# Attention and a feed-forward block on one core: the first stage keeps the feed-forward of one chunk only, and all other chunks run by seven products

## The chip, the cores and the metric

The kernel runs on one core of a Trainium2 chip. The metric is the device time of one launch in microseconds; the median of three runs before the change is 1090.41 us (1090.18 to 1091.8).

## The reference, cut to what matters

```python
# 8 batches x 8 heads x 576 tokens, head_dim 64, 128 features; all fp32
def phi(x):
    proj = np.einsum('bhsd,df->bhsf', x, w_phi)
    proj = proj - np.max(np.abs(proj), axis=-1, keepdims=True)
    return np.concatenate([np.exp(proj), np.exp(-proj)], axis=-1)
q_p, k_p = phi(q), phi(k)
kv  = np.einsum('bhsf,bhsd->bhfd', k_p, v)
z   = np.sum(k_p, axis=2)
num = np.einsum('bhsf,bhfd->bhsd', q_p, kv)
den = np.einsum('bhsf,bhf->bhs', q_p, z)[..., None] + 1e-06
x   = (num / den) as 4608 tokens x 512          # heads side by side
h   = x @ w_in                                  # 512 x 2048
g   = np.maximum(h, 0.0) + alpha * np.minimum(h, 0.0)
out = g @ w_out                                 # 2048 x 512
```

## The kernel before, in words

**Attention.** Work goes by head pairs, 32 of them (`attention_units`, i = 0 to 31): 576 tokens of two heads, keys and queries side by side as nine blocks of 128 tokens. Per pair TensorE projects to 128 features (`project`, L357, tiles `pj` and `pl`: 18 matmuls, each run as two instructions, as all fp32 matmuls here but the transposes), VectorE finds the largest magnitude of each token and subtracts it (L361, L362, result `t`), ScalarE takes both exponentials (L375, L370 for keys). TensorE then sums the key features with a matrix of ones (`k_z`, L415) and multiplies them with v (`k_acc`, L398), both into one PSUM tile `kv`; ScalarE copies it out (`ks`), TensorE transposes it (`kt`, L430), ScalarE copies it (`sf`). Query features are transposed (`q_turn`, L444 and L441, tiles `qt`), and ScalarE takes their exponentials on the way out of PSUM (`qf`, L454, L452). Numerator and denominator are matmuls of `sf` with `qf` (`num`, L463; `den`, L481). The denominator goes through DRAM: row `d9`, reciprocal on VectorE (L500), `rec_d`, a broadcast load `rr`; GpSimd multiplies (L513), and the result is stored to `x_d`.

For the first nine pairs (`ZP`) the sum over tokens takes 20 matmuls with ones. From pair 9 on VectorE first adds the features of the token blocks (`k_sum`, L384, L388, L391, tiles `y` and `z`), and four matmuls are left.

**Precision.** Feed-forward operands are split into a high part and a rest (`rnd`, L154; `low`, L158), so each product is three matmuls (high x high, rest x high, high x rest) of 128 x 128 weights and 512 tokens. The weights arrive as 64-bit words: 32 blocks (16 tiles of d_ff, in and out), each taken apart by ScalarE (scale), four VectorE operations (L206, L207, L213, L214), a GpSimd addition (L218), a ScalarE cast and a GpSimd subtraction.

**Feed-forward.** 4608 tokens are nine chunks of 512. A chunk and one d_ff tile of 128 cost 4 x 3 matmuls up and 4 x 3 down when done plainly. Stage 1 does four of the 16 tiles (`NF1`) plainly for every chunk; chunks 0 to 6 are spread between the attention of later pairs (`ffn1_units`), and the partial outputs go to `part_d` in DRAM. After the last pair comes a stretch of plain work: chunk 0's other twelve tiles (`up2`, `down2`, weights loaded back from DRAM, tile `wd`) and the four tiles of chunks 7 and 8. The last stage takes chunks 1 to 8 in four pairs of chunks and the remaining twelve tiles in pairs (`unit`, `down_pair`): a 2 x 2 block product by seven products and not eight, 42 matmuls up and 42 down for two tiles and two chunks. Its operands are sums and differences of activation blocks (`prepare`, `piece`, tiles `xo`; `operand`, tiles `hv`) and of weight blocks (`sums`: stored to `us_d`, `vs_d`). `sums` reads the decoded weights back from `a_d` and runs on VectorE, after attention.

**What sets the order.** TensorE, SyncE's DMA queue, VectorE and ScalarE follow a list `todo` of (time, function), sorted by hand-tuned times (`places`, `F0` to `U10`, one unit is one pair); after attention the list binds TensorE and SyncE, and in the last stage TensorE, SyncE and GpSimd.

Of the kernel before, what the change touches and what calls it, by code (L numbers as in the profile page):

```python
# [61 lines left out]
ZP = 9


def places(i):
    early = i < ZP
    end = i >= NPAIR - 2
    first = {}
    if i == 0:
        first = dict(  # L70
            kz=0.6087, ka=0.708, ko=0.7486, kr=0.9934, kc=1.4482,
            n=1.9214, q=(0.8813, 0.8308, 0.8837), qe=(0.9994, 1.6727, 0.9984),
        )
    if i == 1:
        first = dict(kz=0.0042, ka=0.0046, ko=0.005)
    return dict(
        ld=-2.0487,
        lv=-0.6714,
        p=(-0.9958 if early else -0.997, -0.2212),
        pl=-0.2217,  # L80
        ke=(-0.1643, -0.0046),
        ks=(-0.1042, 0.1628, 0.3174),
        kz=0.9909,
        ka=1.0012,
        ko=1.0069,
        kr=1.0717,
        kc=1.1318,
        q=(1.4145, 1.4146, 1.3876),
        qe=(1.416, 1.4689, 1.4006),
        d=1.9929,  # L90
        ds=2.0026,
        n=2.0048,
        s=2.0313,
        d9=2.3018,
        dv=2.7654 if early else 2.9056 if end else 2.6473,
        rd=2.9221 if early else 3.2095 if end else 2.7929,
        rr=3.2932 if early else 3.4567 if end else 2.924,
        x=3.3204 if early else 3.4698 if end else 3.4373,
        xs=3.799 if early else 3.7869 if end else 3.541,
    ) | first  # L100


F0 = 9.2903
FR = 3.3778
FB = 8.0905
FL = 1.3973
FX = (1.1204, 0.6722, 0.1849, 0.3895)
FX0 = (1.6389, 1.8451, 1.1996, 0.5009)
FX1 = (0.7187, 0.4692, 0.2819, 0.3079)
FL0 = 2.0983  # L110
FG = (0.1212, 0.3467, 0.482)
GL = (0.3336, 0.4933, 0.5782)
GT = (0.1537, 0.1934, 0.4757)
GE = (0.2092, 0.3109, 0.5393)
# [1066 lines left out]
```

## Time and profile before

| | |
|---|---|
| median of three runs | 1090.41 us |
| the profiled execution, first to last instruction | 1086.2 us |
| TensorE busy | 1060.3 us (98%) |
| VectorE busy | 814.3 us (75%) |
| ScalarE busy | 622.8 us (57%) |
| GpSimd busy | 248.2 us (23%) |
| moved by DMA | 252.18 MB |

The page states no time of the profiled execution besides its span; the median of the runs stands 4.2 us above it. Busy times are unions of an engine's records, so matmuls that overlap count once, and the mean of one matmul is longer than the step from one start to the next. The attention stage with its interleaved feed-forward ends near 477 us, the last seven-product stage begins at 614 us.

### The profile page before, as it was taken

What the parts mean: (1) busy time and instruction counts of PE and PEld (TensorE: products, weight loads), DVE (VectorE), ACT (ScalarE), POOL (GpSimd) and SP (SyncE); (2) the same over time, 40 slices, a digit from 0 to 9 for tenths busy, and PEclk for the clock granted to TensorE, in tenths of its full rate; (3) what the DMA queues carried; (4) which work ended last, traced back from release to release, by engine and by line L of the source; (5) the groups of instructions that cost most, each with busy time, mean ns of one, the idle gap of its engine ahead of it and who ended that gap; (6) DMA issues with size and microseconds to landing.
All of it is one profiled execution on the core that took longest, in us unless ns stands there. A gap on an engine that the chain in (4) does not pass through costs nothing. (4 is left out here: it accounts for less than half of the span.)

```text
span 1086.2 us, 18393 instructions
## 1 busy us (share of the span) xinstructions
PE 1060.3 (98%) x6958; PEld 815.2 (75%) x6958; DVE 814.3 (75%) x1204; ACT 622.8 (57%) x1177; POOL 248.2 (23%) x251
## 2 busy tenths in 40 slices
PE   8999999999999999989897999999999999999998
PEld 6767677677667766767676877888888888888886
DVE  7877889798898988563655578975697669766784
ACT  5777676686667767654544446553565346444542
POOL 1334152424334352442411001012001200020001
PEclk9999999999999999989998999999999999999999
DMA  5576556657666675679579689487657756675555
GB/s 187 184 225 174 152 193 206 228 189 255 192 213 231 219 239 177 199 265 376 185 251 361 249 300 403 161 307 262 225 216 264 276 211 248 223 279 209 193 179 179
DMA packets 97703, 252.18 MB, mean 232 GB/s; under 512 B 17616, under 2 KB 18000, under 8 KB 92240
## 3 DMA queue, kind: packets, MB, share of 16 engines
q1 hardware_dynamic: 84400, 197.46, 53.4%
q0 software_dynamic: 12928, 53.48, 13.6%
q8 instruction: 55, 0.90, 0.3%
q14 instruction: 32, 0.26, 0.1%
q10 hardware_dynamic: 288, 0.07, 0.0%
HBM read 190.91 MB, written 59.92 MB: 231 GB/s over the span
## 5 line engine op out<-in xcount | busy, mean ns | idle before, releaser
L154 ACT CAST hv<-g 128x512 fp32r<-128x512 f32 x168 | 103.8, 622 | 88.6 <-DVE hv L158 29.8
L158 DVE TENSOR_TENSOR hv<-g,hv 128x512 fp32r<-128x512 f32 x168 | 114.4, 688 | 38.5 <-ACT hv L154 38.1
L361 DVE TENSOR_REDUCE m<-pj 128x8 f32<-128x1024 f32 (+1 forms) x66 | 78.3, 1187 | 32.6 <-PE pj L357 32.4
L806 POOL DMA_DIRECT2D out_dram<-pt x33 | 18.0, 547 | 356.7 <-DVE pt L935 355.0
L513 POOL TENSOR_TENSOR s<-s,rr 128x576 f32<-128x576 f32 x32 | 46.7, 1461 | 159.7 <-DMA rr<-rec_d 113.7
L362 DVE TENSOR_TENSOR t<-pj,m 128x1024 f32<-128x1024 f32 (+1 forms) x66 | 78.7, 1192 | 3.3 <-ACT s L474 0.5
L281 DVE SCALAR_TENSOR_TENSOR g<-r,aln,g 128x512 f32<-128x512 f32 x48 | 43.3, 902 | 44.4 <-ACT g L277 44.2
L921 PE MATMUL qa<-hv,wv 128*128 128x512 f32 x192 | 74.8, 390 | 0.0
L919 PE MATMUL qa<-hv,wv 128*128 128x512 f32 x192 | 74.7, 389 | 0.0
L920 PE MATMUL qa<-hv,wv 128*128 128x512 f32 x192 | 74.7, 389 | 0.0
L357 PE MATMUL pj<-w_sb,raw 64*128 64x128 f32 x1024 | 71.7, 279 | 2.1 <-DVE t L362 1.2
L357 PEld LDWEIGHTS pj<-w_sb,raw 64*128 64x128 f32 x1024 | 62.6, 188 | 14.3 <-issue 11.8
L454 ACT ACTIVATE qf<-qt 128x512 f32<-128x512 f32 x128 | 68.7, 618 | 1.4 <-PE qt L444 1.4
L463 PE MATMUL n<-qf,sf 128*64 128x288 f32 x512 | 69.0, 412 | 0.0
L375 ACT ACTIVATE xk<-t 128x1024 f32<-128x1024 f32 x64 | 64.9, 1077 | 5.2 <-DVE t L362 5.2
L218 POOL TENSOR_TENSOR aw<-ew,aw 128x512 f32<-128x512 f32 x32 | 44.6, 1394 | 89.4 <-DVE ew L214 89.4
L563 PE MATMUL o<-gh,w 128*128 128x512 f32 x144 | 62.0, 430 | 2.7 <-ACT gh L154 2.5
L565 PE MATMUL o<-gl,w 128*128 128x512 f32 x144 | 58.6, 407 | 4.4 <-DVE gl L158 4.2
L398 PE MATMUL kv<-xk,v 128*64 128x256 f32 x512 | 62.3, 385 | 0.0
L554 PE MATMUL h<-xh,w 128*128 128x512 f32 x144 | 60.4, 419 | 0.0
L564 PE MATMUL o<-gh,w 128*128 128x512 f32 x144 | 58.1, 404 | 0.0
L474 ACT COPY s<-n 128x288 f32<-128x288 f32 x64 | 25.1, 400 | 56.1 <-PE n L463 42.4
(193 smaller groups left out, 2816.7 us busy)
## 6 DMA issues: line engine op xcount, KB each, us to landing
ws<-us_d SPq DMA_DIRECT2D x24, 1024.0 KB
wv<-vs_d SPq DMA_DIRECT2D x32, 768.0 KB
wv<-v_d SPq DMA_DIRECT2D x24, 768.0 KB
raw<-kq_dram SPq DMA_DIRECT2D x31, 576.0 KB
wa<-u_d SPq DMA_DIRECT2D x24, 512.0 KB
v<-v_dram SPq DMA_DIRECT2D x32, 320.0 KB
xr<-x_d SPq DMA_DIRECT2D x10, 1024.0 KB
rr<-rec_d SPq DMA_DIRECT2D x64, 144.0 KB
```

What stands on the lines that cost most here:

```text
L154: return act.copy(dst, src)
L158: return eng.tensor_tensor(dst, src, f(hi), op=ALU.subtract)
L357: pe.matmul(dst[h, j], lhsT=c["raw"][hs, ts], rhs=w_sb[hs], start=True, stop=True)
L361: dve.tensor_reduce(m, src, axis=AX.X, op=ALU.max, apply_absolute_value=True)
L362: dve.tensor_tensor(t[:, hs, js], src, m.unsqueeze(3).broadcast_to([P, nh, nj, FD]), op=ALU.subtract)
L375: act.activation(x[:, a], c["t", 0], AF.Exp, scale=sg)
L398: pe.matmul(c["kv"][h * D : (h + 1) * D, 0:2], lhsT=c["v"][:, tp, h, :], rhs=c["x", ch][:, :, h, j, :], start=tp == 0, stop=tp == NV - 1,)
L454: act.activation(c["qf"][:, h, a, : 4 * P], ps.rearrange("p j f -> p (j f)"), AF.Exp, scale=sg)
L463: pe.matmul(ps[h * D : (h + 1) * D, :], lhsT=c["st"][:, a, h * D : (h + 1) * D], rhs=c["qf"][:, h, a, u * HS : (u + 1) * HS], start=a == 0 ...
L919: pe.matmul(ps, lhsT=wh, rhs=xh, start=first, stop=False, skip_group_check=True)
L920: pe.matmul(ps, lhsT=wl, rhs=xh, start=False, stop=False, skip_group_check=True)
L921: pe.matmul(ps, lhsT=wh, rhs=xl, start=False, stop=end, skip_group_check=True)
```

## The change

- Stage 1 keeps the feed-forward of chunk 0 alone, with all 16 tiles (`first_chunk`): 32 visits of twelve matmuls (one tile up, or two output blocks of a tile pair down), in slots 8 to 28; even slots have two visits, odd ones one (`SL`). A slot is the work between two projections. Outputs are added up in SBUF by VectorE (`down0_out`). The stretch between attention and the last stage, `part_d`, `a_d` and the plain weights read back are gone.
- Chunks 1 to 8 run all 16 tiles, eight units for a chunk pair and not six, by seven products. Weight sums for all eight are made on GpSimd during attention, as soon as a block pair is decoded (`sum_two` to `sum_rest`), and stored by SyncE.
- In a slot TensorE does one burst of 36 projection instructions of the next pair, one visit of 128x32 matmuls (ones, v, numerator of the pair before, denominator: `k_acc` and `num` now write 32 rows at a time), and one run of transposes. The projected queries are centred and transposed in the slot of their projection. `k_sum` is gone.
- The projection's `pl_0`, the last query transposes `q2` and the denominator share one PSUM bank (tag `a`); `kv` and `kt` share one; `num` uses the bank pair of the keys' projection.
- GpSimd now follows the list too; `places` is replaced by one table of offsets (`OFF`, in fourteenths of a slot, for slots with no, one and two visits) and `PE_AT` for TensorE. In the last stage there are five `hv` tiles (`NH`), and weights arrive for two units at a time in five buffers.

```diff
-NF1 = 4
-NF2 = NF - NF1
-NU = NF2 // 2
+NU = NF // 2
...
-NH = 6
+NH = 5
...
+SL = [sl for sl in range(8, 29) for _ in range(2 - sl % 2)]
+DS = [sl for sl in range(26) for _ in range(2 if sl in (8, 10, 12, 14, 16, 18) else 1)]
...
+PE_AT = dict(pk=0.0, kz=2.0, ka=3.0, n=5.2, d=7.15, kr=8.1, q=8.4, f0=9.95, f1=12.7)
...
+    def sum_two(u, z):
...
+        pool.tensor_tensor(a22, a21, a22, op=ALU.add)
+        pool.tensor_tensor(a21, a11, a21, op=ALU.subtract)
+
+    def sum_four(u, z):
+        _, a11, a12, a21, a22 = wst["s", u, z]
+        pool.tensor_tensor(a11, a22, a11, op=ALU.subtract)
+        pool.tensor_tensor(a12, a12, a11, op=ALU.subtract)
...
+    def sum_rest(u, z):
...
+        low(pool, dst[:, :, 1], st[0], dst[:, :, 0])
...
+        def project():
+            for ch in range(2):
+                p2 = c["pj", ch] = ps_pj.tile([P, 2, 4, FD], F32, tag=f"p{ch}", name=f"pj{i}_{ch}")
+                for j in range(4):
+                    for h in range(2):
+                        project_one(p2[:, h, j], h, 5 * ch + j)
+            c["pl"] = [
+                ps_m.tile([P, 1, 1, FD], F32, tag="a", name=f"pl{i}_0"),
+                psf.tile([P, 1, 1, FD], F32, tag=ftag(1), name=f"pl{i}_1"),
+            ]
+            for h in range(2):
+                project_one(c["pl"][h][:, 0, 0], h, 4)
...
         def k_acc():
             for tp in range(NV):
                 ch, j = divmod(tp, 4)
-                for h in range(2):
+                for g in range(4):
+                    h, e = divmod(g, 2)
                     pe.matmul(
-                        c["kv"][h * D : (h + 1) * D, 0:2],
-                        lhsT=c["v"][:, tp, h, :],
+                        c["kv"][32 * g : 32 * g + 32, 0:2],
+                        lhsT=c["v"][:, tp, h, 32 * e : 32 * e + 32],
                         rhs=c["x", ch][:, :, h, j, :],
...
-            if i < ZP:
-                zs = [c["x", 0][:, :, :, j, :] for j in range(4)] + [c["x", 1][:, :, :, 0, :]]
-            else:
-                zs = [c["z"]]
+            zs = [c["x", 0][:, :, :, j, :] for j in range(4)] + [c["x", 1][:, :, :, 0, :]]
...
+        put(i - 1, "pk", project)
+        put(i - 1, "mk", lambda: centre_four(0))
+        put(i - 1, "mq", lambda: centre_four(1))
+        put(i - 1, "mt", centre_tails)
...
+        put(i - 1, "q", q_turn)
+        put(i - 1, "qe", q_exp)
+        put(i, "kz", k_z)
+        put(i, "ka", k_acc)
...
+        put(i + 1, "n", num)
+        put(i + 1, "d", den)
...
+    def down0_out(u, m):
+        if u == 0:
+            o0[m] = cat.tile([P, C2], F32, name=f"os0_{m}")
+            act.copy(o0[m], cur[m])
+            return
+        dve.tensor_tensor(o0[m], cur[m], o0[m], op=ALU.add)
...
+    def first_chunk():
+        order = [("u", 0), ("u", 1)]
+        for k in range(NU - 1):
+            order += [("u", 2 * k + 2), ("d", k, 0), ("u", 2 * k + 3), ("d", k, 2)]
+        order += [("d", NU - 1, 0), ("d", NU - 1, 2)]
...
+    pinned = {et.PE, et.SP, et.DVE, et.Activation, et.Pool}
```

**TensorE, one pair without feed-forward.** Before, from one sum with ones to the next (`xk` and `k` are key features, `raw` the loaded tokens):

```order
L415 MATMUL kv_964<-xk_805,ones 32x128 x16
L415 MATMUL kv_964<-k_1_138,ones 32x128 x4
L481 MATMUL d_985<-qf_908,sf_892 32x288 x8
L398 MATMUL kv_964<-xk_805,v_750 64x256 x8
L398 MATMUL kv_964<-k_1_138,v_750 64x256 x2
L357 MATMUL pj_0_1011<-w_sb,raw_812 128x128 x8
L463 MATMUL n_0_1023<-qf_908,sf_892 64x288 x4
L463 MATMUL n_1_1028<-qf_908,sf_892 64x288 x4
L430 MATMUL kt_1038<-ident,ks_1033 128x128 x3
L441 MATMUL qt_2_1054<-ident,t_1_780 128x128 x2
L444 MATMUL qt_0_1061<-ident,t_1_780 128x128 x4
L444 MATMUL qt_1_1066<-ident,t_1_780 128x128 x4
```

And now, from one projection to the next:

```order
L370 MATMUL pj_0_322<-w_sb,raw_184 128x128 x8
L370 MATMUL pj_1_331<-w_sb,raw_184 128x128 x8
L370 MATMUL pl_0_340<-w_sb,raw_184 128x128
L370 MATMUL pl_1_341<-w_sb,raw_184 128x128
L428 MATMUL kv_349<-xk_281,ones 32x128 x16
L428 MATMUL kv_349<-k_1_129,ones 32x128 x4
L414 MATMUL kv_349<-xk_281,v_163 32x256 x16
L414 MATMUL kv_349<-k_1_129,v_163 32x256 x4
L479 MATMUL n_404<-qf_246,sf_346 32x288 x16
L496 MATMUL d_437<-qf_246,sf_346 32x288 x8
L443 MATMUL kt_450<-ident,ks_448 128x128 x3
L458 MATMUL qt_1_455<-ident,t_1_425 128x128 x4
```

The projection, which stood in two places with 128x64 matmuls between, is one burst; all matmuls of 32 columns follow one another; the transposed queries (`t_1_425`) are those of the burst at the head of the same slot.

**VectorE, the beginning of a slot with two visits, now** (`g_6`, `gl_6` are chunk 0's activation and its rest, `os` its output, `m` the magnitudes, `a` a weight block):

```order
L308 SCALAR_TENSOR_TENSOR g_6_3099<-r_6_3098,aln,g_6_3099 128x512
L610 TENSOR_TENSOR os_0_2171<-o_2_0_3139,os_0_2171 128x512
L388 TENSOR_REDUCE m_0_3255<-pj_0_3174 128x8
L389 TENSOR_TENSOR t_0_3254<-pj_0_3174,m_0_3255 128x1024
L388 TENSOR_REDUCE m_1_3279<-pj_1_3183 128x8
L389 TENSOR_TENSOR t_1_3278<-pj_1_3183,m_1_3279 128x2x512
L388 TENSOR_REDUCE m_2_3289<-pl_0_3192 128x1
L389 TENSOR_TENSOR t_1_3278<-pl_0_3192,m_2_3289 128x128
L388 TENSOR_REDUCE m_3_3292<-pl_1_3193 128x1
L389 TENSOR_TENSOR t_1_3278<-pl_1_3193,m_3_3292 128x128
L161 TENSOR_TENSOR gl_6_3316<-g_6_3099,gh_6_3204 128x512
```

All centring of a pair stands in one piece behind the addition of the last output block and ahead of the remaining feed-forward and weight work of the slot.

**GpSimd, about one slot with two weight blocks, now** (`e` and `a` are the parts of a weight block, `wo` its split form, `sd` the split sums, `s` a pair's numerator):

```order
L161 TENSOR_TENSOR sd_1_2879<-a_1_2454,sd_1_2879 128x4x256
L228 TENSOR_TENSOR a_0_2629<-e_0_2921,a_0_2629 128x512
L228 TENSOR_TENSOR a_1_2871<-e_1_2924,a_1_2871 128x512
L161 TENSOR_TENSOR wo_0_3036<-a_0_2629,wo_0_3036 128x2x256
L161 TENSOR_TENSOR wo_1_3038<-a_1_2871,wo_1_3038 128x2x256
L528 TENSOR_TENSOR s_2478<-s_2478,rr_2977 128x576
L256 TENSOR_TENSOR a_0_2629<-a_0_2629 128x256
L257 TENSOR_TENSOR a_0_2629<-a_0_2629 128x256
```

Before, GpSimd had the additions, the split and the multiplication here; the sums (L256, L257 and `sd`) stood on VectorE after attention.

## Rows read from the trace of the kernel before

**Rows 1.** The page's first line and its line of busy time: busy us, share of the span, instructions of each engine.

```profile
span 1086.2 us, 18393 instructions
PE 1060.3 (98%) x6958; PEld 815.2 (75%) x6958; DVE 814.3 (75%) x1204; ACT 622.8 (57%) x1177; POOL 248.2 (23%) x251
```

**Rows 2.** Busy time of each engine by stretch: stretch in us from the span's start, its length, then busy us and instructions of TensorE, its weight loads, VectorE, ScalarE and GpSimd; the granted clock of TensorE as a share of full speed; the DMA engines' share; GB/s.

```profile
0.00:42.74 42.74, 38.55 (x477) 28.98 (x478) 33.83 (x58) 25.50 (x52) 9.49 (x15) 1.00 0.58 188
42.74:95.62 52.88, 52.88 (x708) 37.40 (x706) 41.77 (x66) 40.54 (x88) 23.11 (x18) 1.00 0.66 205
300.00:400.00 100.00, 100.00 (x878) 70.02 (x878) 90.40 (x120) 69.80 (x142) 39.32 (x27) 1.00 0.70 222
477.00:490.00 13.00, 8.96 (x25) 5.99 (x24) 8.20 (x11) 3.74 (x7) 6.51 (x6) 0.74 0.59 205
535.00:545.00 10.00, 7.14 (x23) 4.77 (x21) 6.72 (x8) 5.17 (x9) 6.53 (x6) 0.83 0.51 171
583.00:595.00 12.00, 5.57 (x17) 4.15 (x16) 7.22 (x12) 3.64 (x6) 1.24 (x2) 0.72 0.95 346
614.00:1081.20 467.20, 464.46 (x2042) 382.34 (x2040) 349.96 (x553) 232.17 (x395) 40.97 (x74) 1.00 0.68 244
```

**Rows 3.** TensorE's timeline over one pair without feed-forward: start in us, duration of the merged group, line, operation, tiles, shape, count.

```profile
42.74 1.08 PE L415 MATMUL kv<-xk,ones 128*32 128x128 f32 x32
...
43.86 1.15 PE L481 MATMUL d<-qf,sf 128*32 128x288 f32 x16
44.94 1.95 PE L398 MATMUL kv<-xk,v 128*64 128x256 f32 x16
...
47.25 1.16 PE L357 MATMUL pj<-w_sb,raw 64*128 64x128 f32 x16
48.34 2.16 PE L463 MATMUL n<-qf,sf 128*64 128x288 f32 x16
50.43 0.55 PE L430 MATMUL kt<-ident,ks 128*128 128x128 f32 x3
...
52.00 0.49 PE L357 MATMUL pl<-w_sb,raw 64*128 64x128 f32 x4
...
53.32 0.32 PE L415 MATMUL kv<-xk,ones 128*32 128x128 f32 x4
```

**Rows 4.** The same timeline over a later pair: from its numerator to the next one's, with the first and the last of the 24 feed-forward matmuls between, and the step with ones.

```profile
246.04 2.16 PE L463 MATMUL n<-qf,sf 128*64 128x288 f32 x16
...
248.43 0.48 PE L563 MATMUL o<-gh,w 128*128 128x512 f32 x1
...
256.45 0.39 PE L565 MATMUL o<-gl,w 128*128 128x512 f32 x1
256.77 0.43 PE L415 MATMUL kv<-z,ones 128*32 128x128 f32 x8
257.02 1.15 PE L481 MATMUL d<-qf,sf 128*32 128x288 f32 x16
...
261.50 0.71 PE L463 MATMUL n<-qf,sf 128*64 128x288 f32 x4
```

**Rows 5.** The same timeline in the seven-product stage: two matmuls ten starts apart.

```profile
700.28 0.39 PE L919 MATMUL qa<-hv,wv 128*128 128x512 f32 x1
...
702.55 0.39 PE L920 MATMUL qa<-hv,wv 128*128 128x512 f32 x1
```

**Rows 6.** The same timeline behind two of TensorE's waits (in brackets the idle time before the matmul and what ended it): the first and the last of thirteen matmuls behind one of them, and the first behind another.

```profile
482.95 0.80 PE L565 MATMUL o<-gl,w 128*128 128x512 f32 x1 [3.15 <-DVE gl L158]
...
488.23 0.56 PE L565 MATMUL o<-gl,w 128*128 128x512 f32 x1
...
590.53 0.77 PE L563 MATMUL po<-gh,wd 128*128 128x512 f32 x1 [6.43 <-DMA wd<-v_d]
```

**Rows 7.** Groups of VectorE and ScalarE instructions by line and shape: line, engine, operation, tiles, shape, count, busy us in total, mean ns of one, and the engine's idle time before them with what ended it.

```profile
L158 DVE TENSOR_TENSOR hv<-g,hv 128x512 fp32r<-128x512 f32 x168 | 114.4, 688 | 38.5 <-ACT hv L154 38.1
L281 DVE SCALAR_TENSOR_TENSOR g<-r,aln,g 128x512 f32<-128x512 f32 x48 | 43.3, 902 | 44.4 <-ACT g L277 44.2
L158 DVE TENSOR_TENSOR gl<-g,gh 128x512 fp32r<-128x512 f32 x48 | 36.7, 767 | 12.1 <-ACT gh L154 12.0
L207 DVE SCALAR_TENSOR_TENSOR aw<-raww,aw 128x512 uint32<-128x512 uint32 x32 | 26.3, 822 | 1.1
L388 DVE TENSOR_TENSOR z<-y 128x512 f32<-128x512 f32 x23 | 25.8, 1124 | 0.1
L214 DVE SCALAR_TENSOR_TENSOR ew<-raww,ew 128x512 f32<-128x512 uint32 x32 | 22.2, 692 | 1.1
L206 DVE TENSOR_SCALAR aw<-aw 128x512 uint32<-128x512 uint32 x32 | 21.5, 673 | 13.8 <-ACT aw L198 12.7 <-DMA part_d<-os 1.1
L213 DVE TENSOR_SCALAR ew<-aw 128x512 uint32<-128x512 uint32 x32 | 16.3, 511 | 3.0 <-DVE aw L207 0.5
L454 ACT ACTIVATE qf<-qt 128x512 f32<-128x512 f32 x128 | 68.7, 618 | 1.4 <-PE qt L444 1.4
```

**Rows 8.** The same for GpSimd's addition of weight parts.

```profile
L218 POOL TENSOR_TENSOR aw<-ew,aw 128x512 f32<-128x512 f32 x32 | 44.6, 1394 | 89.4 <-DVE ew L214 89.4
```

More of the change, by code (lines that the diff above doesn't have):

```diff
@@ L57 @@
 RAW_BUFS = 2
-S_BUFS = 2
-GB = 5
-XR_BUFS = 1
+S_BUFS = 4
 QH_BUFS = 2
[L62 to L100, printed above, removed]
@@ L103 @@
[L103 to L114, printed above, removed]
-TL = 31.4
-WL = dict(load=-1.1556, scale=-0.4743, split=-0.0175, rest=0.0884, add=0.3177, high=0.7022, low=0.9429, store=1.0847)
-FS = (0.0611, 0.2856)
-GV = 0.4491
-WT = dict(load=-0.63, scale=-0.2464, split=-0.0569, rest=0.0013, add=0.3952, high=0.6164, low=0.8038, store=1.0429)
@@ L256, in fused_kernel, with decode_at @@
     )
-    def decode_at(t, blk):
-        return [(t + (WT if t < TL else WL)[k], lambda u=u: u(*blk, WD)) for k, u in stages.items()]
-    inplace = {(ff, z) for ff in range(NF1) for z in range(2)}
-    W = {ff: weight_tile(w1p, f"w{ff}")[0] for ff in range(NF1)}
-    last = [None]
-    newest = {}
-    def behind(eng):
-        return tc.issue_after(newest[eng].ins)
+    def decode_at(sl, turn, ff, z):
+        for k, u in stages.items():
+            put(sl - (k == "load") + (k == "store"), k, lambda u=u: u(ff, z), turn)
+        if ff % 2:
+            for n, (u, ds) in enumerate(((sum_two, 1), (sum_four, 1), (sum_high, 1), (sum_rest, 1), (sum_store, 1))):
+                put(sl + ds, f"sum{n}", lambda u=u: u(ff // 2, z), turn)
     def act_g(ps, ff, n, gp, rg, bufs, tag, el, g_bufs=G_BUFS):
@@ new lines, in down0, with out0 @@
+    def down0(u, m, two):
+        cur[m] = ps = bank0(m + 1, two, f"o0_{u}_{m}")
+        for r in range(2):
+            gemm2(ps, weights_of(2 * u + r, 1), m, *gq[2 * u + r], r == 0, r == 1)
+    def down0_out(u, m):
[4 more added lines that the diff above has]
+        dve.tensor_tensor(o0[m], cur[m], o0[m], op=ALU.add)
+    def out0(m):
+        nc.sync.dma_start(out[m * P : (m + 1) * P, :C2], o0[m])
@@ L918, in three @@
+    for n in range(16):
+        put(29, f"pt{n}", lambda n=n: (prep.extend(prepare(1) if n == 0 else []), pieces(1)))
+    for u in range(2):
+        put(29, f"lu{u}", lambda u=u: load_up(1, u))
     def three(ps, wh, wl, xh, xl, first, end):
@@ L995, in end @@
             leaky(st["a"], g[1, 0], f2, f"21_{tag}")
-        return begin, second, rest, end
+        return begin, second, rest, end, begin_b
     hv, wv = {}, {}
```

823 lines of the change are left out of this document (336 added, 487 removed).

## The prediction

> **What bounds the kernel now.** I read the share of each engine first, then busy time by stretch, then TensorE's timeline of single pairs, and the vector and GpSimd groups last. The page gives a span of 1086.2 us with TensorE busy for 1060.3 of it [rows 1]. That alone does not say that TensorE sets the time, since matmuls overlap in the records; the stretches do. From 42.74 to 95.62 and from 300 to 400 TensorE is busy without a break at full clock, while VectorE stands at 79% and 90%, ScalarE at 77% and 70%, GpSimd at 44% and 39% [rows 2]. So the attention stage is a queue of matmuls with no hole in it, and so is nearly all of the seven-product stage (464.46 of 467.2 us). The holes are between the two: in three stretches of 13, 10 and 12 us TensorE idles 4.0, 2.9 and 6.4 us, and the granted clock falls to 0.74, 0.83 and 0.72 [rows 2]. Behind a wait of 3.15 us for the low half of an activation, thirteen matmuls start from 482.95 to 488.23, 0.44 us apart, at the lower of the clock's two levels; the third hole begins with 6.43 us for weights from DRAM [rows 6]. At full clock they lie 0.227 us apart: ten starts between 700.28 and 702.55 [rows 5]. A gain must therefore come from fewer matmul columns, fewer changes of tile shape, or these holes.
>
> The unit of the sum is what one head pair costs on TensorE. A pair without feed-forward takes 10.58 us (kv at 42.74 to kv at 53.32) [rows 3]. A later pair takes 15.46 us (n at 246.04 to n at 261.50) with 24 feed-forward matmuls in it (the first at 248.43, the last at 256.45) [rows 4], so 15.46 - 24 x 0.227 = 10.01 of its own.
>
> **Fewer feed-forward matmuls.** A chunk and d_ff tile costs 24 wide matmuls plainly; the seven products cost 84 for two chunks and two tiles, 21 each. Before: 9 x 4 x 24 + 12 x 24 = 1152 plain and 4 x 6 x 84 = 2016. Now: 16 x 24 = 384 plain and 4 x 8 x 84 = 2688. That is 96 fewer, and all run end to end: 96 x 0.227 = **-21.8 us**.
>
> **The normaliser by matmul again.** Pairs 9 to 31 summed the features on VectorE and needed 8 short matmuls; now all need 40. The step takes 0.25 us with 8 (256.77 to 257.02) [rows 4] and 1.12 with 40 (42.74 to 43.86) [rows 3]: 23 x 0.87 = **+20.0 us**. VectorE loses three additions per pair, the second of them at 1.12 us [rows 7]; that buys no time by itself.
>
> **Fewer changes of shape.** The first order excerpt shows what is merged. Before, a pair changes the shape of its matmuls six times: d to kv with v, to projection, to n, to transposes, to projection, to kv with ones [rows 3]; now three times. Three insertions of feed-forward matmuls in a later pair cost 10.01 - (10.58 - 0.87) = 0.30, so 0.10 a change. The columns streamed stay the same, since kv with v and n, two at a time before, become twice the instructions at four at a time, as d is. I take 0.14 for each of the three changes saved, because narrow shapes met each other there, hence 10.15 us for a slot without feed-forward. Bounds: 10.58 if nothing is saved, 9.9 if each costs twice that. Against that, a later pair before would have cost 10.01 + 0.87 = 10.88 with all 40 short matmuls; a slot now has one block of feed-forward instead of three. So 9 early pairs give 9 x (10.15 - 10.58) = -3.9 and 23 later ones 23 x (10.15 + 0.05 - 10.88) = **-15.6 us**. With the normaliser, attention as a whole comes out at +0.5 us. One wait is added: the tails of the projection now use the PSUM bank that holds the last query transposes of the pair before, so they wait for its exponentials. From tail to tail that is 6.6 us of matmuls (the rest of the burst's seam, then kv, n and d), 0.8 of transposes, four exponentials at 0.54 (68.7 / 128) [rows 7], the two short ones and the hand-overs, 10.3 us; a slot with a visit has room for it, the ten without do not: **+1.5 us** (0 to +5).
>
> **The stage between goes.** Chunks 7 and 8 no longer have a plain part and chunk 0's last twelve tiles move into the pairs' slots, so the three holes go: 13.3 us of idle time [rows 2] and about thirty of the 65 matmuls in them at 0.44 instead of 0.227 [rows 2, 5, 6], 6 us, with 0.7 us of single waits: **-20 us**. What is late next? Three places wait once. At the start the transposes of pair 0 stand ahead of the projections of pair 1 on TensorE, so it waits for about 6 us of centring, and may lose its clock as at 482.95 [rows 6]; before, it idled 4.2 us in its first 42.74 [rows 2], so I add 3 (0 to 6). Chunk 0's input is fetched right behind the store of pair 3, and two casts stand in ScalarE's queue for it: 2 (0 to 4). At the turn to the products, pair 1's fourteen operands (0.6 to 1.4 us each on two engines) stand between the last pairs' copies, and VectorE's queue holds the reciprocals of pairs 30 and 31, which wait for DMAs, ahead of operands of the first unit: 3 (0, or the 6.4 + 2 of the old weight wait). Together **+8 us**.
>
> **What costs nothing, and its cover.** The weight sums move from VectorE in the second stage to GpSimd in the first, their stores from GpSimd's queue to SyncE's; the reloads and the partial outputs of stage 1 disappear. They are needed only in the seven-product stage, so their cover is whole slots, as long as GpSimd keeps up. A slot with two visits lasts 10.15 + 24 x 0.227 + 0.1 = 15.7 us. GpSimd has 4.62 us a pair with one weight block (23.11 / 5) [rows 2]; a second block adds some 3 us (one addition 1.39, one subtraction like it) [rows 8]; the sums are four 256-wide and one 1024-wide operations, between 4.2 us (cost by width from 1.39 at 512) and 7.6 (the narrow ones at 1.2, the wide one at 2.8): 12 to 15 us. VectorE has 8.35 us a pair (41.77 / 5), plus a second block of 2.70 (0.67 + 0.82 + 0.51 + 0.69), plus 0.90 and 0.77 for an activation, plus two additions at 0.69 [rows 2, 7]: 14.1 us, 90%, the share at which TensorE had no hole from 300 to 400. ScalarE issues 22 operations there; it took 0.49 us each in that stretch (69.8 / 142): 11 us. SyncE gets 16 more large stores and loses 36; one waiting store could hold a load behind it for a few us, which the two spare input tiles cover.
>
> **Sum** against the profiled execution's span: 1086.2 - 21.8 + 20.0 - 3.9 - 15.6 + 1.5 - 20 + 8 = 1054.4 us. The median of the runs, 1090.41, is 4.2 above that span, and I add the same: **1059 us**.
>
> **Rivals.**
> (a) GpSimd and VectorE slow each other and the two-visit slots become theirs. For it: the subtraction for gl takes 0.77 us where hv's, with GpSimd nearly idle, takes 0.69, and the addition z, of the same width, 1.12 [rows 7]; GpSimd's share in these slots doubles to about 85%. If the 7 us of SBUF operands in such a slot go by z's ratio instead of gl's (1.63 / 1.11), VectorE needs 17.4 us, 1.7 too many in each of 11 slots: 1059 + 19 = 1078, up to 1090 if the other visited slots follow. Against it: that is the worst of three rows. The Trainium skill (GPSIMD Engine Reference, Key points) says that GpSimd shares its SBUF interfaces with VectorE and contends with instructions that have two SBUF inputs; by that rule the move of the sums works against this change, and the three rows agree in direction.
> (b) Slower: the transposes wait in every slot. Before, a pair's queries were transposed more than a slot after their projection; now projection, 5.65 us of VectorE work (8.35 - 2.70) and transposes lie in one slot (first and second excerpt). TensorE reaches the transposes about 9.0 us after the burst begins (10.15 less some 1.2 of the 1.57 between 50.43 and 52.00 [rows 3]); the centring ends about 7.4 us after it when VectorE is on time (1.1 for the first half of the burst, 5.65, and the hand-overs). If VectorE starts it more than 1.6 us late, TensorE waits for the rest; the kernel is slower than before once the wait exceeds 32 / 31, 1.0 us in each slot. At 2.4 us a slot it is 1059 + 74 = 1133, more if the clock falls. For it: VectorE takes its work in the order written, and an addition of chunk 0's output stands ahead of the centring. Against it: a 90% VectorE leaves more than that free.
> (c) The seven-product stage starves: operand buffers go from six to five. One wait of 0.5 us per product and pair is 28 x 0.5 = 14: 1073. Against it: with fewer partial sums to add, VectorE's work per product falls, and before it idled TensorE 2.7 us in 467 [rows 2].
> (d) The change does not do what it says: the thirty-two-wide kv and n run two at a time, not four. Then a pair costs 2.2 + 1.9 us more (the kv and n steps of [rows 3] doubled): 1059 + 32 x 4.1 = 1190. Against it: d, in that shape, takes 1.08 us for 16 instructions of 288 columns, half of n's 2.09.
>
> **Chances.** Forecast 0.70 (1043 to 1068: each one-time wait between its ends, the slot between 9.9 and 10.4); (a) 0.14; (c) 0.05; (b) 0.09, of which 0.07 end above 1092.6 and 0.02 within 0.2%, about what can be told from no change; (d) 0.02. Faster: 0.70 + 0.14 + 0.05 = 0.89; same 0.02; slower 0.09. The range 1043 to 1085 takes in the forecast, most of (a) and (c).
>
> **What will show it.** n starts 10.2 to 10.4 us apart without a visit, 12.9 with one, 15.7 with two, TensorE without idle time there; the first seven-product matmul near 430 us; four pairs of 152.4 us each; at most 8 us of idle time at start, slot 8 and turn. Wrong if transposes wait on VectorE in most slots, if GpSimd is above 95% in the two-visit slots, or if the visit of thirty-two-wide matmuls takes more than 6.5 us.

## The result and the profile after

The changed kernel takes 1051.95 us (median of four runs, 1049.69 to 1058.26) against 1090.66 for the kernel before: ratio 0.9657, 95% interval 0.9629 to 0.9685. It is 3.4% faster; the forecast was 1059. Its profiled execution took 1052.68 us, with a span of 1050.9 where the sum had 1054.4.

The page's first line and its line of busy time, which answer to [rows 1]:

```profile
span 1050.9 us, 21876 instructions
PE 1032.1 (98%) x8750; PEld 815.3 (78%) x8750; DVE 733.0 (70%) x1133; ACT 615.0 (59%) x1129; POOL 245.5 (23%) x226
```

Busy time by stretch, columns as in [rows 2]: start, last slots without a visit, slots 6 to 8, ten visited slots, the turn to the products, the products.

```profile
0.00:42.74 42.74, 35.99 (x526) 28.58 (x530) 28.50 (x44) 26.43 (x49) 9.78 (x17) 0.92 0.60 198
42.74:80.90 38.16, 38.16 (x669) 28.24 (x664) 28.97 (x46) 31.73 (x62) 23.54 (x20) 1.00 0.79 249
80.90:120.20 39.30, 36.78 (x559) 26.52 (x555) 31.67 (x52) 29.84 (x60) 22.95 (x19) 1.00 0.81 254
120.20:261.93 141.73, 141.73 (x1954) 106.19 (x1950) 118.11 (x179) 104.35 (x207) 96.14 (x77) 1.00 0.80 262
425.00:450.00 25.00, 22.80 (x136) 15.58 (x128) 19.92 (x28) 12.62 (x24) 6.05 (x5) 1.00 0.65 208
450.00:1045.60 595.60, 593.83 (x2613) 489.94 (x2611) 395.10 (x613) 303.59 (x517) 20.05 (x35) 1.00 0.61 210
```

In the visited slots TensorE is busy without a break, VectorE for 83% and GpSimd for 68%. The holes of [rows 2, 6] between the stages, at half clock, are gone; what idles lies mostly at the start, in slots 6 to 8 and at the turn. Before the last product only the start still falls to half clock: the granted clock was 0.50 from 10.24 to 17.07, behind TensorE's longest wait, and the projection in that stretch took 3.10 us where the one of the slot shown further down takes 2.06:

```profile
12.55 1.94 PE L458 MATMUL qt<-ident,t 128*128 128x128 f32 x8 [4.69 <-DVE t L389]
...
14.84 3.10 PE L370 MATMUL pj<-w_sb,raw 64*128 64x128 f32 x32
```

TensorE's longest waits as a list (who waits for what: us in total, times, longest):

```profile
PE qt L458 <- DVE t L389: 6.2, 3, 4.7
PE pa L753 <- ACT u L765: 2.1, 3, 1.2
PE q L461 <- ACT ds L506: 1.0, 1, 1.0
```

TensorE's timeline over one slot without a visit, from numerator to numerator, answers to [rows 3]:

```profile
40.13 2.12 PE L479 MATMUL n<-qf,sf 128*32 128x288 f32 x32
42.07 1.15 PE L496 MATMUL d<-qf,sf 128*32 128x288 f32 x16
43.16 0.55 PE L443 MATMUL kt<-ident,ks 128*128 128x128 f32 x3
43.54 1.04 PE L458 MATMUL qt<-ident,t 128*128 128x128 f32 x8
...
44.73 2.06 PE L370 MATMUL pj<-w_sb,raw 64*128 64x128 f32 x32
...
47.06 1.08 PE L428 MATMUL kv<-xk,ones 128*32 128x128 f32 x32
...
48.17 1.91 PE L414 MATMUL kv<-xk,v 128*32 128x256 f32 x32
...
50.33 0.67 PE L479 MATMUL n<-qf,sf 128*32 128x288 f32 x8
```

It takes 10.20 us where [rows 3] had 10.58. The numerator's 32 instructions take 1.94 us (40.13 to 42.07), less than the 2.09 of the 16 before: four at a time run, not two. Numerators over a slot with two visits (133.01 to 148.55, 15.54) and one with one visit (148.55 to 161.36, 12.81), which answer to [rows 4]:

```profile
133.01 2.12 PE L479 MATMUL n<-qf,sf 128*32 128x288 f32 x32
...
148.55 2.12 PE L479 MATMUL n<-qf,sf 128*32 128x288 f32 x32
...
161.36 2.12 PE L479 MATMUL n<-qf,sf 128*32 128x288 f32 x32
```

Groups of VectorE and GpSimd (columns as in [rows 7]) that answer to [rows 7, 8]; the third is a new one, the rest of the weight sums:

```profile
L224 DVE SCALAR_TENSOR_TENSOR e<-raw,e 128x512 f32<-128x512 uint32 x32 | 28.0, 876 | 1.1
L228 POOL TENSOR_TENSOR a<-e,a 128x512 f32<-128x512 f32 x32 | 46.3, 1448 | 114.0 <-DVE e L224 111.7 <-DMA raw<-kq_dram 2.3
L161 POOL TENSOR_TENSOR sd<-a,sd 128x1024 fp32r<-128x1024 f32 x16 | 38.1, 2381 | 31.7 <-ACT sd L157 26.5 <-PE pj L370 5.2
L161 DVE TENSOR_TENSOR hv<-g,hv 128x512 fp32r<-128x512 f32 x224 | 153.3, 693 | 73.7 <-ACT hv L157 73.3
```

### The profile page after: what moved, and what is told of

Its sections match the earlier page's. It is cut to its first block, busy times and chain, and to the rows that moved or that the text cites. A ratio compares the mean times of both kernels' runs of the same rounds, so it can differ in the third digit from the quotient of the medians.

```text
span 1050.9 us, 21876 instructions
## 1 busy us (share of the span) xinstructions
PE 1032.1 (98%) x8750; PEld 815.3 (78%) x8750; DVE 733.0 (70%) x1133; ACT 615.0 (59%) x1129; POOL 245.5 (23%) x226
## 5 line engine op out<-in xcount | busy, mean ns | idle before, releaser
L157 ACT CAST hv<-g 128x512 fp32r<-128x512 f32 x224 | 139.2, 623 | 123.0 <-DVE hv L161 60.4
L161 DVE TENSOR_TENSOR hv<-g,hv 128x512 fp32r<-128x512 f32 x224 | 153.3, 693 | 73.7 <-ACT hv L157 73.3
L388 DVE TENSOR_REDUCE m<-pj 128x8 f32<-128x1024 f32 x64 | 78.0, 1219 | 47.9 <-PE pj L370 47.9
L755 PE MATMUL qa<-hv,wv 128*128 128x512 f32 x256 | 99.7, 390 | 0.0
L754 PE MATMUL qa<-hv,wv 128*128 128x512 f32 x256 | 99.7, 389 | 0.0
L753 PE MATMUL qa<-hv,wv 128*128 128x512 f32 x256 | 99.7, 389 | 0.0
L389 DVE TENSOR_TENSOR t<-pj,m 128x1024 f32<-128x1024 f32 x64 | 78.4, 1225 | 4.6
L228 POOL TENSOR_TENSOR a<-e,a 128x512 f32<-128x512 f32 x32 | 46.3, 1448 | 114.0 <-DVE e L224 111.7
L479 PE MATMUL n<-qf,sf 128*32 128x288 f32 x1024 | 68.0, 406 | 0.0
L773 ACT ACTIVATE r<-g 128x512 f32<-128x512 f32 x65 | 37.6, 625 | 50.1 <-DVE g L769 49.8
L414 PE MATMUL kv<-xk,v 128*32 128x256 f32 x1024 | 61.1, 379 | 0.0
L755 PEld LDWEIGHTS qa<-hv,wv 128*128 128x128 f32 x256 | 48.1, 188 | 10.0
L754 PEld LDWEIGHTS qa<-hv,wv 128*128 128x128 f32 x256 | 48.1, 188 | 10.0
L753 PEld LDWEIGHTS qa<-hv,wv 128*128 128x128 f32 x256 | 48.1, 188 | 9.9
```

Source lines behind the costliest of these rows:

```text
L157: return act.copy(dst, src)
L161: return eng.tensor_tensor(dst, src, f(hi), op=ALU.subtract)
L388: dve.tensor_reduce(m, src, axis=AX.X, op=ALU.max, apply_absolute_value=True)
L389: dve.tensor_tensor(dst, src, m.unsqueeze(3).broadcast_to([P, nh, nj, FD]), op=ALU.subtract)
L414: pe.matmul(c["kv"][32 * g : 32 * g + 32, 0:2], lhsT=c["v"][:, tp, h, 32 * e : 32 * e + 32], rhs=c["x", ch][:, :, h, j, :], start=tp == 0, ...
L479: pe.matmul(ps[32 * g : 32 * g + 32, :], lhsT=c["st"][:, a, 32 * g : 32 * g + 32], rhs=c["qf"][:, g // 2, a, u * HS : (u + 1) * HS], start ...
```

## Experiments on the terms of the sum

Theory: TensorE's own work sets the time from end to end, and the change pays by what it takes out of it. Rivals: other engines or operands share the bound, or the gain comes from one place. Differences below are to the changed kernel's median of 1051.95 where nothing else is said; the kernel before, run again beside each experiment, had medians from 1089.74 to 1090.7.

**More matmuls (e3_more_products).** The small product rest x rest is added, in all of chunk 0's visits (`gemm1`, and likewise `gemm2`) and in the third to fifth of the seven products for every second tile pair (`three`):

```diff
+            pe.matmul(ps, lhsT=wl, rhs=xl, start=False, stop=False)
...
+        if more:
+            pe.matmul(ps, lhsT=wl, rhs=xl, start=False, stop=False, skip_group_check=True)
```

> The changed kernel with extra matmuls of rest x rest: four in each of chunk 0's 32 visits (128), and 24 in each of the four pairs of chunks (96). Theory (TensorE is the bound in both stages, 0.227 us a matmul): 128 x 0.227 = 29.1 us more in the attention stage and 96 x 0.227 = 21.8 more in the seven-product stage, 1051.9 + 50.9 = 1103. Rival for the seven-product stage (it waits for operands or weights, and matmuls only fill the waits): under 10 us there. Rival for the attention stage (VectorE or GpSimd hold the visited slots): under 15 us there.

Measured: 1103.62, 51.7 more than the changed kernel. Slots with two visits are 17.35 us long and not 15.53, with one 13.72 and not 12.81: 0.2275 us for each of the 8 and 4 matmuls. From the last numerator but one to the end it is 650.6 us and not 628.7, 21.9 more. TensorE is the bound in both stages. The products do wait for operands, 2.1 us for `u` in the list above, but the added matmuls do not fill these waits.

**Sum with ones on TensorE, alone (b1_no_ksum).**

```diff
         def k_sum(step):
-            if i < ZP:
-                return
+            return
...
-            if i < ZP:
+            if i < NPAIR:
```

> The kernel before the change, but all pairs sum the key features by 40 short matmul instructions; VectorE's three additions of pairs 9 to 31 are gone and nothing else moves. Theory (this part of the change costs what its matmuls take): 23 x 0.87 = 20.0 us more than before, 1110.6. Rival (VectorE at 90% was already late there, and its freed 3 us a pair give something back): 1095 to 1105.

Measured: ratio 1.017 (1.015 to 1.019), by that ratio 18.5 us more; later pairs are 16.33 us long and not 15.46, the 0.87 of the term, and from the first numerator to the last it is 20.1 us longer. VectorE, at 62% between 300 and 400 us and not at 90% [rows 2], gave nothing back.

**Quarters, alone and undone (b2_quarter, e1_wide64).** b2 makes the second form of the first on the kernel before, e1 the first of the second on the changed kernel, for the numerator likewise:

```diff
-                for h in range(2):
+                for g in range(4):
+                    h, e = divmod(g, 2)
                     pe.matmul(
-                        c["kv"][h * D : (h + 1) * D, 0:2],
-                        lhsT=c["v"][:, tp, h, :],
+                        c["kv"][32 * g : 32 * g + 32, 0:2],
+                        lhsT=c["v"][:, tp, h, 32 * e : 32 * e + 32],
```

> The kernel before the change, but the product of key features and v and the numerator are made 32 rows at a time, with twice the instructions; the order stays. Theory (a change of tile shape costs 0.10 to 0.14 us): the denominator and the product with v now have one shape, the numerator still stands between two other shapes, so one change less a pair: 32 x (0.10 to 0.14) = 3 to 4.5 us less than before, 1086 to 1087.5. Rival (quarters run two at a time and not four): 32 x 4.1 us more. Second rival (no effect): 1090.6.

> The changed kernel with the product of key features and v and the numerator 64 rows wide again, as before the change; everything else stays. Theory (each change of tile shape costs TensorE 0.10 to 0.14 us, and TensorE sets every slot): two more changes in each of 32 slots, so 32 x 2 x (0.10 to 0.14) = 6 to 9 us more than the changed kernel's 1051.9, 1058 to 1061; numerators without a visit between 10.4 and 10.5 us apart instead of 10.2. Rival (the merging of the two projection pieces gives the whole gain, quarters are worth nothing): 1052 and 10.2 apart. Second rival (64-wide matmuls of this kind are cheaper than quarters, which need twice the instructions): below 1050.

Measured: b2 has ratio 0.9964 (0.9948 to 0.9979), by that ratio 3.9 us less; early pairs take 10.41 and not 10.58, later ones 15.31 and not 15.46. e1 takes 1058.47, 6.5 us more than the changed kernel, and its slots are 0.29 longer, visited or not (the sum is less than 32 times that, since its slots 6 and 7 lost 1.1 us to waits and those of the changed kernel 3.3):

```profile
39.91 2.11 PE L478 MATMUL n<-qf,sf 128*64 128x288 f32 x16
...
50.39 2.11 PE L478 MATMUL n<-qf,sf 128*64 128x288 f32 x16
```

One change of shape less is worth 0.15 to 0.17, two are worth 0.29: 0.15 each, a little above the 0.10 to 0.14. That it is the change of shape and not the quarters themselves, b2 shows: its numerator, still between two other shapes, takes 2.08 us from its start to the next group's, before 2.09 [rows 3], while its denominator, now followed by its own shape, takes 0.97, before 1.08.

```profile
48.20 2.15 PE L464 MATMUL n<-qf,sf 128*32 128x288 f32 x32
50.28 0.55 PE L431 MATMUL kt<-ident,ks 128*128 128x128 f32 x3
...
54.28 1.15 PE L482 MATMUL d<-qf,sf 128*32 128x288 f32 x16
55.25 1.91 PE L399 MATMUL kv<-xk,v 128*32 128x256 f32 x32
```

The Trainium skill (TensorEngine Tiling (Array Packing), Key Properties) says that changing the tiling mode drains TensorE; these runs agree and give the price. Of the 0.38 us that a slot without a visit lost (10.58 to 10.20), e1's two changes are 0.29; the merged projection is left with 0.09.

## Experiments on what was said to cost nothing

**Weight sums on VectorE (e2_sums_dve).**

```diff
-        pool.tensor_tensor(a22, a21, a22, op=ALU.add)
+        dve.tensor_tensor(a22, a21, a22, op=ALU.add)
...
-        low(pool, dst[:, :, 1], st[0], dst[:, :, 0])
+        low(dve, dst[:, :, 1], st[0], dst[:, :, 0])
```

> The changed kernel with the sums of weight blocks (four 256-wide and one 1024-wide operation per pair of blocks, 16 pairs) on VectorE instead of GpSimd, in the same places of the order. Theory (GpSimd is the cover: VectorE has no room for them in slots with two weight blocks): about 0.4 x 4 + 1.25 = 2.9 us of VectorE a pair of blocks; two slots of 28.35 us together held 23.6 us of VectorE work and would hold 23.6 + 1.5 x 2.9 = 28.0, 99%, so TensorE waits in slots 8 to 19: 3 to 15 us more than the changed kernel, 1055 to 1067. Rival (VectorE has room enough and the move to GpSimd bought nothing, or VectorE gets faster by more when GpSimd rests): 1050 to 1052, TensorE without idle time in slots 8 to 19.

Measured: 1069.52, 17.6 more, a little beyond the theory's range. The stretch from 120.20 to 261.93 there:

```profile
120.20:261.93 141.73, 134.49 (x1842) 98.34 (x1837) 136.15 (x199) 96.67 (x188) 52.30 (x37) 1.00 0.74 240
```

VectorE is at 96% and TensorE idles 7.2 us. From the ninth numerator to the 22nd it is 12.5 us longer, within the theory; the rest lies where the theory had nothing, in slots without a visit (two take 11.8 us and not 10.2) and at the turn (a wait of 4.4 us for `xo`). The move to GpSimd is a part of the gain that the sum had at nothing: with the sums on VectorE in the same places, 17.6 of the 38.7 us go.

**Centring late (e6_late_centre).**

```diff
         def centre_four(ch):
+            for n in range(2 if ch == 0 else 0):
+                m = wk.tile([P, 2, 4], F32, tag="m2", name=f"m2{i}_{n}", bufs=2)
+                dve.tensor_reduce(m, c["pj", 0], axis=AX.X, op=ALU.max, apply_absolute_value=True)
```

> The changed kernel with two idle 1024-wide reductions on VectorE ahead of each pair's centring, 2.45 us more a slot. Theory (the centring has a margin of about 1.6 us before the transposes wait): slots without a visit grow by 0.8 us, 11 x 0.8 = 9; in slots 8 to 19 VectorE needs 23.6 + 4.9 = 28.5 us for two slots of 28.35, 0 to 3 us more; together 1060 to 1064. Rival (there is no margin, every microsecond of lateness goes to TensorE): 32 x 2.45 = 78 more, 1130. Second rival (more margin than 3 us): 1052.

Measured: 1094.06, 42 more, far beyond the theory. With 2.45 us more on VectorE, slots without a visit take 11.06 on average (10.83 to 10.91 and 11.25 in turn, 0.86 more) and with one 13.55 (0.74 more), but slots with two take 17.4 (1.9 more). So, by subtraction, the margin is 1.6, 1.7 and 0.55 us. In the visited slots VectorE was busy for only 87% (123.34 of 142.00 us from 120 to 262), and still TensorE waited for it: its share does not tell the margin of one result in its queue. TensorE's waits for the centring, as a list:

```profile
PE n L482 <- DVE t L389: 11.8, 22, 1.0
PE d L499 <- DVE t L389: 8.9, 11, 0.8
```

What waits here is not the transposes but the numerator and the denominator, which stand ahead of them: the numerator writes the bank pair that the keys' centring reads, the denominator the bank of a projection's tail.

## Experiments with more work off TensorE

**Half of the key sum on GpSimd (e4_half_sum).**

```diff
+        def k_half():
+            x = c["x", 0].rearrange("p a h n f -> p (a h) (n f)")
+            y = wk.tile([P, 4, 2 * FD], F32, tag="y", name=f"y{i}", bufs=1)
+            pool.tensor_tensor(y, x[:, :, : 2 * FD], x[:, :, 2 * FD :], op=ALU.add)
...
-PE_AT = dict(pk=0.0, kz=2.0, ka=3.0, n=5.2, ...
+PE_AT = dict(pk=0.0, kz=6.5, ka=3.0, n=5.2, ...
```

> The changed kernel, but GpSimd adds the first two of the four full token blocks of the key features to the last two (one 1024-wide addition a pair, from pair 1 on), the sum with ones needs 24 matmul instructions instead of 40 and stands behind the numerator, and v has two buffers. Theory (TensorE sets every slot, GpSimd has room): 31 x 16 x 0.027 = 13.5 us less than the changed kernel, 1038.5; GpSimd's share in slots 10 to 19 goes from 68 to 85%, numerators without a visit 9.8 apart. Rival (contention: what GpSimd does slows VectorE): VectorE's two-input operations grow by 20% and more, TensorE waits in the slots with two visits, 1045 to 1065.

Measured: 1097.28, 45 more; the theory fell. Rows of GpSimd, VectorE, ScalarE and TensorE around 42 us, each from its own engine's timeline:

```profile
41.31 2.37 POOL L413 TENSOR_TENSOR y<-xk 128x1024 f32<-128x1024 f32 x1 [2.16 <-PE kv L436]
43.63 0.91 POOL L257 TENSOR_TENSOR a<-a 128x256 f32<-128x256 f32 x1
...
41.73 2.23 DVE L217 TENSOR_SCALAR a<-a 128x512 uint32<-128x512 uint32 x1
...
47.69 1.04 ACT L158 CAST sd<-a 128x1024 fp32r<-128x1024 f32 x1 [5.13 <-POOL a L263]
...
49.64 0.69 PE L469 MATMUL q<-ident,t 128*128 128x128 f32 x2 [5.97 <-ACT ds L514]
50.26 3.70 PE L371 MATMUL pj<-w_sb,raw 64*128 64x128 f32 x32
```

Three things are to be seen. The addition waits in GpSimd's queue for the pair before to release `y`; the weight sums wait behind it, ScalarE's cast of them stands ahead of the denominator's copy, and TensorE waits 5.97 us for the PSUM bank that this copy frees. And VectorE's `a`, 0.41 us when alone, takes 2.23: it ends 0.28 us after GpSimd's addition. And behind the wait the clock falls: the projection takes 3.70 us and not 2.06. The mean granted clock of e4's execution is 0.979, that of the changed kernel 0.995; by these shares of the spans (an estimate: 0.021 x 1096 less 0.005 x 1051) up to 18 of the 45 us are the clock.

**Key sum on VectorE, where it has room (e8_late_sum, e9_more_sum).** Of e8; e9 has the even pairs from 10 on as well:

```diff
+        def k_fold(n):
+            x = c["x", 0].rearrange("p a h n f -> p (a h) n f")
...
+            dve.tensor_tensor(y, x[:, :, 0] if n == 1 else y, x[:, :, n], op=ALU.add)
...
+        if i >= 20:
+            for n in range(1, 4):
+                put(i - 1, "ky", lambda n=n: k_fold(n))
```

> The changed kernel, but for pairs 20 to 31 VectorE adds up the four full token blocks of the key features (three 512-wide additions a pair, where a slot has at most one weight block), the sum with ones then needs 16 matmul instructions and not 40, and stands behind the numerator for all pairs. Theory (TensorE is the bound; VectorE, at 66% there, has room for 2.1 us a pair, and additions on VectorE hold up nobody): 12 x 24 x 0.027 = 7.8 us less, 1044; in slots 20 to 28 the numerators are 0.65 closer, 14.9 and 12.2. Rival (VectorE's centring comes late, as with two idle reductions more): no gain or a loss, 1050 to 1058.

> As the run with late sums, and the same for the even pairs from 10 to 18, whose additions lie at the end of slots with one visit. Theory (VectorE 83% there, 91% with 2.1 us more in two slots): 17 x 0.65 = 11 us less than the changed kernel, 1041. Rival (the margin of the centring in slots with two visits, 0.5 us by the run with idle reductions, is used up): slots 10 to 19 get longer, 1045 to 1055.

Measured: 1085.77 and 1089.6, 34 and 38 more; both theories fell. In early slots, where nothing is added, e8 takes 10.54 and 11.49 in turn: the sum with ones behind the numerator is itself too late for the copies that follow (ScalarE waits 2.39 us for it). In late slots numerators wait up to 4.4 us for the centring, and the clock falls behind these waits too (means 0.988 and 0.987, by the same estimate 8 and 9 us). VectorE and GpSimd there (e8):

```profile
289.77 0.68 DVE L415 TENSOR_TENSOR y<-xk 128x512 f32<-128x512 f32 x1
290.49 4.42 DVE L415 TENSOR_TENSOR y<-y,xk 128x512 f32<-128x512 f32 x2
294.83 1.21 DVE L389 TENSOR_REDUCE m<-pj 128x8 f32<-128x1024 f32 x1
...
290.10 2.59 POOL L162 TENSOR_TENSOR sd<-a,sd 128x1024 fp32r<-128x1024 f32 x1 [4.50 <-ACT sd L158]
292.65 1.71 POOL L162 TENSOR_TENSOR wo<-a,wo 128x512 fp32r<-128x512 f32 x1
```

The first addition takes 0.68; the other two take 4.42 together, the second ending 0.55 us after GpSimd's first instruction and the third 0.55 after its second. The 2.1 us that were to cost nothing became 5.1 ahead of the centring, with a margin of half a microsecond to 1.7.

## Experiments on the one-time waits

**Three repairs (e5_front, e7_front2, e10_front_turn).** All reorder the start: half of pair 1's projection goes ahead of pair 0's transposes; all move casts of chunk 0's input back. e5 moves the reciprocals of all slots without a visit, e7 and e10 that of pair 5 alone; e10 also moves the load of later inputs and gives the denominator's copy `ds` two buffers:

```diff
+        if i == 1:
+            todo.append((-0.5, lambda: project((0,)), "pk", 0, 0))
+            todo.append((0.22, lambda: project((1,)), "pk", 0, 0))
...
+        if i == 5:
+            todo.append((7 + 7.4 * U, invert, "dv", 7, 0))
...
-            pool.dma_start(raw, src)
+            (pool if p == 1 else nc.sync).dma_start(raw, src)
```

> The changed kernel with two repairs of its one-time waits. At the start TensorE does half of pair 1's projection and pair 0's sum with ones before it transposes pair 0's queries, and the other half of the projection behind pair 0's product with v. In slot 7 VectorE takes the reciprocal behind the centring, and ScalarE and VectorE take chunk 0's first two casts behind the exponentials of the queries. Theory (these waits lie on TensorE's path): the second pair's transposes start at 18 to 20 us instead of 23.1, 3 to 4.5 us less at the start, and 2.5 to 3.3 less at slots 6 and 7, 1044 to 1046.5. Rival (TensorE waits as long a few steps later): 1051 to 1052.

> As the first repair of the start and of slots 6 and 7, but VectorE's reciprocal goes behind the centring for pair 5 alone (there it had been moved for the last pairs too, and with it their multiplication on GpSimd and the load that is issued behind it), and VectorE takes all four low parts of chunk 0's input behind the centring of slot 8. Theory (the wait of 6.57 us at the turn came from the reciprocals, that of 2.55 us in slot 8 from the low parts): numerators up to pair 6's as early as in the first repair (88.95), 3 to 5 us ahead of the changed kernel at the last pair, the turn as in the changed kernel: 1047 to 1049. Rival (another wait takes their place at the turn): 1052.

> As the second repair, with two more steps. The input of later chunk pairs is loaded by SyncE's queue and not by GpSimd's, so that it does not stand between the last pairs' multiplications, and VectorE's first subtraction for pair 2 then stands 19 instructions later, behind pair 1's operands. And the denominator's copy ds has two buffers. Theory (the wait at the turn came from pair 2's subtraction, which stood ahead of pair 1's last operands on VectorE and waited 5.95 us for that load; the wait of 1.34 us in slot 8 came from the single ds): the last pair 3 to 4.5 us ahead of the changed kernel, at the turn under 2.5 us of waits and TensorE at full clock, 1045 to 1048. Rival (the turn waits for the denominators' way through DRAM whatever stands in the queues): 1051 to 1053 again.

Measured: 1058.17, 1053.07 and 1051.33; ratios to before 0.9709 (0.9686 to 0.9731), 0.9655 (0.963 to 0.9681), 0.9644 (0.9618 to 0.967). The start of the second works (first numerator at 27.33 and not 29.94, the last but one at 419.03 and not 422.18), and the turn takes it back. VectorE's and TensorE's rows at the turn of e7:

```profile
432.18 0.73 DVE L749 TENSOR_TENSOR t<-xr 128x512 f32<-128x512 f32 x1 [5.95 <-DMA xr<-x_d]
...
434.29 0.50 PE L770 MATMUL pa<-xo,ws 128*128 128x512 f32 x1 [4.51 <-DVE xo L161]
```

VectorE's first step for pair 2 stands ahead of pair 1's last operands and waits for a load that GpSimd issues behind a multiplication (at 423.70; at 424.95 in the changed kernel): an earlier TensorE only waits there longer. e10 takes that out: from its first numerator to the last but one (31.13 to 420.20) it takes 389.1 us where the changed kernel took 392.2, with no wait in slots 6 to 8, and the wait at the turn is 0.28. Yet its span is 1050.4: in that execution the granted clock was 0.50 from 20.7 to 27.5, where e7's start had none below 1.00; the first numerator came 1.2 us later than in the changed kernel and 3.8 later than in e7, and a wait of 2.0 us for `u` stands in the products. Its interval overlaps that of the changed kernel: that it beats it is not shown. e5's hole at the turn, 6.57 us from one start to the next, has the same place; there the load was issued later still (428.00).

## Why the prediction was right, step by step

- **Fewer feed-forward matmuls, -21.8:** right; e3 measures 0.2275 us each in both stages.
- **Normaliser, +20.0:** right; 0.87 a pair in b1.
- **Fewer changes of shape, -3.9 and -15.6:** right in kind, a little small. A slot without a visit takes 10.20 and not 10.15. With one it takes 12.81 and not 10.15 + 12 x 0.227 + 0.05 = 12.92, with two 15.53 and not 15.70: 10 x 0.11 + 11 x 0.17 = 3.0 us less than forecast, 0.5 more in the others.
- **The tails' bank, +1.5:** mis-sized. TensorE waited for it 0.4 us in all, in two places; it is out by 1.1.
- **The stage between, -20:** no run isolates it, but the trace of the kernel before sizes it. From 476.18 to 615.84 it starts 511 wide matmuls, 116.3 us at 0.2275, and takes 139.66, 23.4 more:

```profile
476.18:615.84 139.66, 125.66 (x513) 99.30 (x512) 74.96 (x113) 62.65 (x108) 32.58 (x43) 0.94 0.79 285
```

As the remainder of the sum it comes out a little smaller. The span fell by 35.3. Of that, -21.8 + 20.0 for the first two terms, 9 x (10.20 - 10.58) = -3.4 for early pairs, -18.3 for later ones (21 visited slots of 14.24 us on average, 18.3 matmuls at 0.2275 in each, leave 10.07 against 10.88; two slots of 10.20), 8.6 for single waits and 0.4 for the bank leave -20.8.

- **Single waits, +8:** right in sum, 8.6, in part by chance. The second numerator came at 40.13, before at 37.76: 2.4, with the wait for the centring and the lost clock that I had named. Slots 6 and 7 lost 3.3 (11.92 + 11.79 against 2 x 10.20). At the turn four starts are 0.98, 1.07, 0.80 and 0.92 apart and not 0.227: 2.9. In slot 7 it was the path forecast: ScalarE's cast waited 2.06 us for chunk 0's input, ahead of the denominator's copy. The path of slot 6 I had not seen: the reciprocal waited 3.19 us for the 4.5 KB row `d9`, which had been issued 7.9 us earlier, shortly after a store of 1 MB of weight sums (69.83) and one of split weights (70.78), and the centring stood behind the reciprocal. That the row stood behind these stores is inferred. In e3 the same two slots lost 0.25 us and in e1 1.1, so the 3.3 are in part this execution's. The rows of SyncE's queue, of VectorE, and of ScalarE one slot later:

```profile
74.37 0.60 SPq L510 DMA_DIRECT2D d<-ds  x1
...
82.27 0.22 DVE L515 RECIPROCAL r<-d 128x9 f32<-128x9 f32 x1 [3.19 <-DMA d<-ds]
...
95.68 1.15 ACT L157 CAST x<-xr 128x512 fp32r<-128x512 f32 x2 [2.06 <-DMA xr<-x_d]
```

- **The median above the span, +4.2:** the step that failed. In all four runs of the changed kernel the time is 1.7 to 1.8 us above the span, and 1.7 to 1.9 in all later runs on record, of whatever kernel; if it was so in the profiled execution before, the other 2.4 were the scatter of that execution. With -3.5 for the span this makes 5.9 of the 7 us between 1059 and 1051.95; most of the rest is that the profiled execution of the changed kernel lies 0.7 above its own median.
- **Rival (a):** its mechanism is real and harder than I priced it, yet it did not decide. Counted over the rows of each trace, 24 VectorE instructions that began while a GpSimd instruction ran took over 0.15 us longer than their form does alone, 17.4 us in all; before it was 54 and 45.6 us, in e4 85 and 84 us. The new order puts most of GpSimd's work beside the centring, which is not held: 130 of its 211 us from 30 to 404 us, before 72 of 164 from 42.74 to 477. GpSimd was busy for 7.6 to 10.4 us of a slot with two visits, not the 12 to 15 of the forecast; part of its work falls into the slot behind.
- **Rival (b):** it did not occur, but my ground against it was wrong. VectorE was as busy as forecast in the slots with two visits (12.2 to 14.3 of 15.5 us up to 262 us, forecast 14.1), yet "a 90% VectorE leaves more than that free" fails there: e6 finds 0.55 us of margin, not 1.6, and at the numerator and the denominator, a wait for PSUM banks that neither the sum nor the rival had, not at the transposes. The rival was near; that it stayed out is in part luck.
- **Rivals (c) and (d)** did not occur (e3 and TensorE busy for 593.83 of 595.60 us of the products; the numerator's 1.94 us).

## What to carry to other kernels

Where a trace shows one engine busy without a break, price a reordering by its counted instructions and shape changes; the slots so priced held within 0.2 us each. A share of 66 or 83% on another engine is no room: ask how late its next result may be, and measure that margin by adding idle work ahead of it, before moving anything there; here a new wait also cost clock behind it. A wait removed early in a chain pays only if no later place waits for something that does not move with it.
